# A 16-head decode block on one core: half a run of K per batch held in two PSUM banks between the layers, with exponents and expanded queries moved into other banks

## The chip, the core and the metric

The kernel runs on one of the eight cores of a Trainium2 chip. The metric is device time in microseconds (us), the median of three runs. An execution that the hardware profiler recorded gives the views that are quoted here; instructions in them carry the kernel's line numbers (L673 is line 673 of the kernel before).

## The reference

Eight sequences (batches) decode one token each through two layers of attention and MLP, all in bfloat16. Both layers use the same weights and the same caches of K and V, so each cache is read by layer 0 and again by layer 1. Cut to what matters:

```python
B, D, Hq, Hkv, Sk, Dh = 8, 448, 16, 8, 4096, 256
def _A_ref(x, k_cache, v_cache, wq, wo):            # k_cache, v_cache: (B, Hkv, Sk, Dh)
    q = (x @ wq).reshape(B, 1, Hq, Dh).transpose(0, 2, 1, 3)
    k = jnp.repeat(k_cache, 2, axis=1)
    v = jnp.repeat(v_cache, 2, axis=1)
    p = softmax(einsum("bhqd,bhkd->bhqk", q, k) * Dh ** -0.5)
    return einsum("bhqk,bhkd->bhqd", p, v).reshape(B, 1, Hq * Dh) @ wo

for layer in range(2):
    x = x + _A_ref(layernorm(x), A_k_cache, A_v_cache, A_wq, A_wo)
    x = x + _B_ref(layernorm(x), B_w1, B_w2, B_w3, B_w4)   # an MLP with two layernorms of its own
```

One head of one batch has 4096 x 256 bf16 of K, 2 MB, and as much of V. Eight batches of eight heads are 134 MB of K and 134 MB of V, and layer 1 of a batch needs layer 0 of the whole batch first.

## The kernel before

**Tiles.** SBUF holds NSLOT = 30 slots of 512 KB (4 KB on each of the 128 partitions). A head's K comes as two *runs* of two neighbouring slots (K_RUN = 2, 1 MB, one DMA); a head's V comes as four chunks of one slot. A run's parts are counted in slots, so its `y` is 0 or 2. K lands with keys on partitions and is transposed in place by VectorE in 32 x 32 blocks of 32-bit words, 128x512 words at a time, four instructions for a run (L673). The same instruction applied twice gives the data back. TensorE multiplies the transposed K by the expanded query `qx` into a score bank (L689, `sc`, 32 matmuls a run), then come the softmax (L697 to L723) and the product with V (L753, `v_phase`).

**Kept K.** `KEPT` counts the runs of each batch that stay in their slots, transposed, from layer 0 to layer 1: nine for batch 0, twelve for each of the others, which is all of heads 2 to 7. Heads 0 and 1 (0 to 3 in part for batch 0) load their K again in layer 1. Twelve runs fill 24 of the 30 slots, and six are left to turn over.

**PSUM.** Eight banks: `psS0`, `psS1` for scores, alternating by head in the order of `k_phase` (`n_k % 2`); `psO0`, `psO1` for the product with V; `psM0`, `psM1` for the tail of layer 0 and of layer 1 (projection, MLP, norms, next query); `psX0`, `psX1`. A head's scores take columns 0 to 255 of its score bank. ScalarE writes the exponents from there into `psX0` (L707), VectorE transposes them in place (L712), ScalarE copies the part that is needed into `ring` (L716). All heads use `psX0` for this, one after the other; it is a *strict* resource, whose next writer waits for all earlier users. The expanded query of a batch (`expand`, L502) is made in `psX1`: 16 small matmuls (L512), then four copies into `qx` on VectorE and ScalarE (L521).

**Order of the loads.** `load_order` (L550) lists them, and SP issues them in that order; each waits until the slots that the planner gave it are free. For batch b it lists the K of heads 0 and 1 of layer 0, run by run, between them the K of heads 0 and 1 of layer 1 of batch b-1 (`fr`), then the K of heads 2 to 7 of layer 0. After each run up to two V chunks of layer 0 follow whose scores are due. Then come the rest of layer 0's V, then the V of layer 1 of batch b-1. In this last stretch the tail of layer 0 of batch b runs (`tail`, L789), whose end gives layer 1 its query, and the kept heads are scored for layer 1 (entries "S", 24 us after the last V of layer 0 and then every 2 us, by the planner's clock), which frees their slots. In the text the *K stretch* of a batch is the time in which its K is loaded, and the *V stretch* the time with V loads alone.

**Order on the engines.** `Graph.schedule` (L161) plays the program with estimated durations and fixes each engine's order. An engine that is free takes the ready task with the lowest priority number, and the number is mostly the due time (`at`) plus a constant. A task that takes a slot can begin when a slot is free. SP's queue is looked at first:

```python
        def can(t):
            if not t.allocs:
                return True
            i = t.allocs[0]
            return len(i.pool.free) >= i.reserve + len(t.allocs) and i.pool.find(len(t.allocs)) is not None
```

A task given as a list and marked `whole` is one entry of an engine's order: its instructions run one after the other, each waiting for the end of the one before. Waits between engines, and between tasks, follow from `reads` and `writes` of named resources (`Res`, L72).

## Time and profile before

| | |
|---|---|
| median of 3 runs | 1133.84 us (1133.22 to 1134.58) |
| the profiled execution | 1133.89 us, of which 1132.1 us from the first to the last instruction (the span) |
| loads of K | 163 of 1024 KB, issue to landing 18.8 us in the median |
| loads of V | 512 of 512 KB, 9.1 us |
| busy | PE 698.0 us, VectorE (DVE) 770.5, ScalarE (ACT) 114.5, GpSimd (POOL) 98.3 |
| transposes of K (L673) | 652, 431.1 us busy, 690 ns each |
| scores (L689) | 8192 matmuls |
| exponents (L707), their transposes (L712), copies (L716) | 128 of each, 448, 450 and 213 ns |

How to read the page: it shows busy time in 40 equal slices of the span, as tenths, one row for each engine, one for the DMA engines and one for the GB/s that they moved. The chain of waits is followed back from the last instruction, at each step to what released it; its shares name the engines and lines on that path. A stretch (window) is given in us from the span's start. "To landing" is the time from a load's issue on SP to its last byte: a long one means that many loads stand ahead of it in the queue, not that the load is slow.

### The profile page before, as it was taken

How to read it: one execution, taken by the hardware profiler on the slowest of the kernel's cores; microseconds unless marked ns; L12 is line 12 of the kernel's file. 1: busy time of each engine (PE TensorE's matmuls, PEld its weight loads, DVE VectorE, ACT ScalarE, POOL GpSimd, SP SyncE). 2: the span in 40 equal slices, each digit the busy share in tenths (PEclk: the TensorE clock that was granted, in tenths of full speed). 3: DMA queues.
4: the chain of work that ended last, by engine and by line, in shares of the span. 5: the costliest groups of instructions: out<-in, count | busy, mean ns of one | idle time of the engine just before them, and what ended most of it. 6: DMA issues, size and time to landing. Idle time of an engine off the chain costs nothing.

```text
span 1132.1 us, 41859 instructions
## 1 busy us (share of the span) xinstructions
PE 698.0 (62%) x18716; PEld 466.5 (41%) x18716; DVE 770.5 (68%) x2704; ACT 114.5 (10%) x434; POOL 98.3 (9%) x269
## 2 busy tenths in 40 slices
PE   2534565685557755577555865568555785557775
PEld 2322443353433543345432554335443354334553
DVE  4955799537994379844996459953798438974463
ACT  0100021001110011101111011100111001110110
POOL 0100021001110011100110011100111001100110
PEclk9999965556555555556555565555655555555555
DMA  9999999999999999999999999999999999999993
GB/s 344 415 412 394 411 417 412 405 384 417 415 412 402 404 415 415 403 404 409 415 414 400 402 413 415 413 397 401 416 415 413 395 410 413 416 395 407 409 408 135
DMA packets 101444, 452.63 MB, mean 400 GB/s; under 512 B 11008, under 2 KB 12944, under 8 KB 80016
## 3 DMA queue, kind: packets, MB, share of 16 engines
q1 hardware_dynamic: 101248, 449.96, 99.0%
q8 instruction: 146, 2.39, 0.9%
q14 instruction: 34, 0.28, 0.1%
q10 hardware_dynamic: 16, 0.01, 0.0%
HBM read 449.91 MB, written 0.01 MB: 397 GB/s over the span
## 4 chain that ended last, share of the span: by engine, by line
DVE 35%; DMA 32%; PE 23%; issue 8%; ACT 1%; SPq 0%; POOL 0%; POOLq 0%; ACTq 0%; DVEq 0%
DMA kv<-in_A_v_cache_dram 28%; DVE kv L673 21%; PE psO L753 8%; PE psS L689 7%; PE psM L493 3%; DMA wo_sb<-in_A_wo_dram 2%; DVE psX L712 2%; DVE small L697 2%; PE psM L783 2%; DMA kv<-in_A_k_cache_dram 2%; DVE oX L758 1%; PE psO L765 1%; DVE oT L772 1%; DVE small L885 1%; PE psM L811 1%
## 5 line engine op out<-in xcount | busy, mean ns | idle before, releaser
L673 DVE STREAM_TRANSPOSE kv<-kv 128x512 int32<-128x512 int32 x652 | 431.1, 690 | 16.7 <-DMA kv<-in_A_k_cache_dram 16.4
L689 PE MATMUL psS<-kv,qx 128*8 128x128 bf16 x8192 | 255.0, 296 | 185.1 <-DVE kv L673 88.2
L753 PE MATMUL psO<-kv,ring 128*2 128x256 bf16 x4096 | 288.6, 396 | 102.8 <-DMA kv<-in_A_v_cache_dram 86.7
L689 PEld LDWEIGHTS psS<-kv,qx 128*8 128x8 bf16 x8192 | 196.9, 115 | 243.8 <-DVE kv L673 118.4
L753 PEld LDWEIGHTS psO<-kv,ring 128*2 128x2 bf16 x4096 | 81.0, 94 | 175.2 <-DMA kv<-in_A_v_cache_dram 138.3
L758 DVE STREAM_TRANSPOSE oX<-psO 128x256 f32<-128x256 f32 x128 | 56.2, 439 | 109.6 <-PE psO L753 109.0
L701 POOL PARTITION_ALL_REDUCE small<-small x128 | 46.7, 365 | 712.1 <-DVE small L699 704.8
L783 PE MATMUL psM<-oT,wo_sb 128*128 128x1 bf16 x2048 | 74.0, 166 | 53.7 <-DVE oT L772 41.2
L707 ACT ACTIVATE psX<-psS,small 128x256 f32<-128x256 f32 x128 | 57.4, 448 | 452.2 <-DVE small L703 397.5
L697 DVE TENSOR_REDUCE small<-psS 128x1 f32<-128x256 f32 x128 | 52.4, 409 | 73.1 <-PE psS L689 55.7
L783 PEld LDWEIGHTS psM<-oT,wo_sb 128*128 128x128 bf16 x2048 | 63.9, 104 | 83.3 <-DVE oT L772 65.5
L772 DVE TENSOR_SCALAR oT<-psO,small 64x4 bf16<-64x4 f32 x256 | 55.3, 216 | 47.7 <-PE psO L765 43.0
L721 POOL PARTITION_ALL_REDUCE small<-small x128 | 51.5, 402 | 272.1 <-DVE small L719 237.5
L712 DVE STREAM_TRANSPOSE psX<-psX 128x256 f32<-128x256 f32 x128 | 57.6, 450 | 11.8 <-ACT psX L707 10.3
L765 PE MATMUL psO<-oX,id 128*32 128x4 f32 x1024 | 36.6, 200 | 27.1 <-DVE oX L758 20.7
L765 PEld LDWEIGHTS psO<-oX,id 128*32 128x32 f32 x1024 | 30.2, 145 | 44.7 <-DVE oX L758 35.6
L836 PE MATMUL psM<-small,w_sb 128*128 128x1 bf16 x896 | 30.2, 166 | 22.6 <-DVE small L828 22.3
L836 PEld LDWEIGHTS psM<-small,w_sb 128*128 128x128 bf16 x896 | 27.0, 104 | 37.7 <-DVE small L828 27.6
L716 ACT CAST ring<-psX 128x64 bf16<-128x64 f32 x128 | 27.2, 213 | 149.2 <-DVE psX L712 149.2
L493 PEld LDWEIGHTS psM<-small,wq_sb 128*128 128x128 bf16 x1024 | 30.7, 104 | 17.6 <-issue 12.9
L493 PE MATMUL psM<-small,wq_sb 128*128 128x1 bf16 x1024 | 34.2, 166 | 2.3 <-DVE small L895 1.8
L811 PE MATMUL psM<-small,w_sb 128*128 128x1 bf16 x896 | 28.7, 165 | 8.9 <-DVE small L895 8.9
(91 smaller groups left out, 353.4 us busy)
## 6 DMA issues: line engine op xcount, KB each, us to landing
kv<-in_A_v_cache_dram SPq DMA_DIRECT2D x512, 512.0 KB, 9.1
kv<-in_A_k_cache_dram SPq DMA_DIRECT2D x163, 1024.0 KB, 18.8
wo_sb<-in_A_wo_dram SPq DMA_DIRECT2D x1, 3584.0 KB, 27.1
wq_sb<-in_A_wq_dram SPq DMA_DIRECT2D x3, 1024.0 KB, 7.5
w_sb<-in_B_w_dram SPq DMA_DIRECT2D x1, 1568.0 KB, 18.1
w_sb<-in_B_w_dram SPq DMA_DIRECT2D x3, 448.0 KB, 16.4
wq_sb<-in_A_wq_dram SPq DMA_DIRECT2D x2, 256.0 KB, 11.6
w_sb<-in_B_w_dram SPq DMA_DIRECT2D x2, 112.0 KB, 14.7
```

Source lines behind the costliest of these rows:

```text
L493: last = e.matmul(M[:, base + col * nb:base + (col + 1) * nb], w, xn[:, :, kx], start=(k == 0), stop=(k == NCC - 1))
L673: return e.transpose(ap, ap)
L689: last = e.matmul(S[32 * j:32 * j + 8, w * y:w * y + w], qx[x][:, h, 2 * c + u, :], kt[:, :, c, 8 * j:8 * j + 8, u], start=(c == 0 and u = ...
L697: g.add("dve", lambda e: e.tensor_reduce(pm[par][:, :], S[:, 0:256], axis=AX.X, op=ALU.max), (0.46, 0.33), pr, reads=[rS], writes=[res(f"p ...
L707: g.add("act", lambda e: e.activation(p_ps.rearrange("p (z k y) -> p y z k", z=8, k=8), S[:, 0:256].rearrange("p (y z k) -> p y z k", y=4, ...
L712: g.add("dve", lambda e: e.transpose(p_ps, p_ps), (0.48, 0.38), pr, reads=[rP], writes=[rP])
L753: last = e.matmul(O[32 * j:32 * j + 2, 0:DH], ring[:, pin.slot, i, 2 * a:2 * a + 2], slot_ap(vin)[:, i * DH:(i + 1) * DH], start=(a == 0 a ...
L758: g.add("dve", lambda e: e.transpose(oX[:, :].rearrange("p (c r) -> p c r", r=32), O[:, 0:DH].rearrange("p (a r k) -> p a k r", a=2, k=4)) ...
L765: last = e.matmul(O[32 * a:32 * a + 32, 256:260], id4[:, :], oX[:, :].rearrange("p (a k r) -> p a k r", a=2, k=4)[:, a % 2, :, a // 2], st ...
L772: g.add("dve", lambda e, j=j: e.tensor_scalar(oT[64 * j:64 * j + 64, jb, 4 * h:4 * h + 4], O[64 * j:64 * j + 64, 256:260], rc_ring[64 * j: ...
L783: last = e.matmul(psM[layer][:, c:c + 1], wo_sb[:, c0:c0 + P], oT[:, jb, kt_:kt_ + 1], start=(first and k == 0 and c == 0), stop=False, sk ...
L836: last = e.matmul(M[:, 64 + c:65 + c], w4_sb[:, c0:c0 + P], hT[:, ft:ft + 1], start=(ft == 0), stop=(ft == NFT - 1))
```

## The change

In layer 0 of batches 1 to 7, head 1's second run has its first slot *stashed*: after the transposes in place, two more 128x512 transposes write the slot's content, as it was loaded, into `psX0` and `psX1`, which together hold exactly one slot. It is a whole task on VectorE with priority `at + 10`. In layer 1 the same two transposes bring it back (transposed, as it is needed) into a slot that VectorE's task takes from the pool, with priority `at`; the load for that run fetches only the other slot, 512 KB in place of 1 MB. The two slots of this run are scored by separate tasks of 32 matmuls with 64 columns.

The exponents move to columns 256 to 511 of the head's own score bank, and the expanded query to columns 256 to 383: of the score bank that is next (layer 0), or of the tail's bank `psM0` (layer 1). The score and tail banks are tracked by quarters of 32 partitions (`quads`), and no bank is strict any more. The heads of layer 1 that load again are ordered from the highest down.

```diff
 WO_AT = 11
+STASH = (0, 1, 1, 1, 1, 1, 1, 1)
 AHEAD = (0, 3, 0, 0, 0, 0, 0, 0, 0)
...
-    R["psX0"] = Res(psum=True, strict=True)
     kv_pool = Pool(NSLOT)
...
         return last
-    g.add("dve", c_dve, 3.0, 0, writes=[res("psO0", True), res("psO1", True), res("psS0", True), res("psS1", True),
-                                        res("psM0", True), res("psM1", True), res("xT"), res("wpad"),
+    def quads(bank):
+        return [res(f"{bank}_{a}", True) for a in range(4)]
+    g.add("dve", c_dve, 3.0, 0, writes=[res("psO0", True), res("psO1", True), quads("psS0"), quads("psS1"),
+                                        quads("psM0"), quads("psM1"), res("xT"), res("wpad"),
                                         res("mask"), res("qx0"), res("qx1")])
...
-    def expand(layer, b, prio):
-        X = psX[1]
-        rX = [res(f"psX1_{a}", True) for a in range(4)]
+    def expand(layer, b, X, rX, prio):
         x = layer
...
                 for a in range(4):
-                    last = e.matmul(X[32 * a:32 * a + 32, 384 + 32 * j:416 + 32 * j], eye[:, i0:i0 + 63:2],
+                    last = e.matmul(X[32 * a:32 * a + 32, 256 + 32 * j:288 + 32 * j], eye[:, i0:i0 + 63:2],
                                     q_sb[:, b, :], start=True, stop=True)
             return last
-        g.add("pe", f, (0.37, 0.2), prio, reads=[res(f"q{b}"), res("const")], writes=rX)
+        g.add("pe", f, (0.37, 0.2), prio, reads=[res(f"q{b}"), res("const")], writes=[rX])
         for a in range(4):
...
                 o = qx[x][32 * a:32 * a + 32, :, :, :].rearrange("p h (c s) x -> p s (h c) x", s=4)
-                i = X[32 * a:32 * a + 32, 384:512].rearrange("p (s hc j) -> p s hc j", s=4, j=2)
+                i = X[32 * a:32 * a + 32, 256:384].rearrange("p (s hc j) -> p s hc j", s=4, j=2)
                 o = o[:, :, :, 2 * a:2 * a + 2]
...
-    expand(0, 0, -100)
+    expand(0, 0, psS[0], quads("psS0"), -100)
...
+    def stashed(b, h):
+        if STASH[b] and h == max(i for i in range(HKV) if kept_runs(b, i) < RUNS):
+            return 2 - 2 * kept_runs(b, h)
+        return None
     class Load:
-        def __init__(self, kind, layer, b, h, part):
-            self.kind, self.layer, self.b, self.h, self.part = kind, layer, b, h, part
+        def __init__(self, kind, layer, b, h, part, n=1):
+            self.kind, self.layer, self.b, self.h, self.part, self.n = kind, layer, b, h, part, n
             self.at = None
...
             nonlocal now
-            now += {"K": K_RUN * P * CHUNK * 2 / RATE, "V": P * CHUNK * 2 / RATE, "S": 0.0}[x.kind]
+            now += x.n * P * CHUNK * 2 / RATE if x.kind != "S" else 0.0
             x.at = now
...
         def fresh(layer, b, h):
-            return [Load("K", layer, b, h, y) for y in range(0, 4, K_RUN)
-                    if layer == 0 or y // K_RUN < RUNS - kept_runs(b, h)]
+            return [Load("K", layer, b, h, *((y + 1, 1) if layer and y == stashed(b, h) else (y, K_RUN)))
+                    for y in range(0, 4, K_RUN) if layer == 0 or y // K_RUN < RUNS - kept_runs(b, h)]
...
             l1 = sorted(range(HKV), key=lambda h: -kept_runs(b - 1, h)) if b else []
-            fr = [h for h in l1 if kept_runs(b - 1, h) < RUNS]
+            fr = sorted((h for h in l1 if kept_runs(b - 1, h) < RUNS), reverse=True)
             ks = []
...
     softmax = {}
-    n_k = n_v = 0
...
         S = psS[par]
-        rS = res(f"psS{par}", True)
-        p_ps, rP = psX[0][:, 0:256], res("psX0", True)
+        rS = quads(f"psS{par}")
+        p_ps = S[:, 256:512]
         x = layer
...
         fresh = RUNS - kept_runs(b, h)
-        kts = []
+        pieces = []
         old = kept.pop((b, h), {})
+        def load(y, n, uses):
+            kin = [Inst(kv_pool, u) for u in uses]
+            rk = Res()
+            loads["K", layer, b, h, y] = dma(lambda e: e.dma_start(slot_ap(kin[0], n), k_run(b, h, y, n)),
+                                             n * P * CHUNK * 2, at, [], writes=[rk], takes=kin)
+            done = []
+            for q in range(2 * n):
+                def tr(e, q=q):
+                    ap = slot_ap(kin[0], n).bitcast(i32)[:, q * 512:(q + 1) * 512]
+                    return e.transpose(ap, ap)
+                rKT = Res()
+                g.add("dve", tr, (0.75, 0.615), at + y, reads=[rk], writes=[rKT])
+                done.append(rKT)
+            return y, kin, done
         for y in range(0, 4, K_RUN):
             if y in old:
-                kts.append(old[y])
+                pieces.append(old[y])
+            elif layer == 1 and y == stashed(b, h):
+                back = Inst(kv_pool, 1)
+                rKT = Res()
+                g.add("dve", [
+                    lambda e, q=q: e.transpose(slot_ap(back).bitcast(i32)[:, q * 512:(q + 1) * 512],
+                                               psX[q][:, :].bitcast(i32)) for q in range(2)
+                ], (0.8, 0.65), at, reads=[res("psX0", True), res("psX1", True)], writes=[rKT], takes=[back],
+                    whole=True)
+                pieces += [(y, [back], [rKT]), load(y + 1, 1, [1])]
             else:
                 keep = layer == 0 and y // K_RUN >= fresh
-                kin = [Inst(kv_pool, 2 if keep else 1) for _ in range(K_RUN)]
-                rk = Res()
-                loads["K", layer, b, h, y] = dma(
-                    lambda e, kin=kin, y=y: e.dma_start(slot_ap(kin[0], K_RUN), k_run(b, h, y, K_RUN)),
-                    K_RUN * P * CHUNK * 2, at, [], writes=[rk], takes=kin)
-                done = []
-                for hf in range(2 * K_RUN):
-                    def tr(e, kin=kin, hf=hf):
-                        ap = slot_ap(kin[0], K_RUN).bitcast(i32)[:, hf * 512:(hf + 1) * 512]
-                        return e.transpose(ap, ap)
-                    rKT = Res()
-                    g.add("dve", tr, (0.75, 0.615), at + y, reads=[rk], writes=[rKT])
-                    done.append(rKT)
-                kts.append((kin, done))
+                stash = layer == 0 and y == stashed(b, h)
+                pieces.append(load(y, K_RUN, [2, 1] if stash else [1 + keep] * K_RUN))
                 if keep:
-                    kept.setdefault((b, h), {})[y] = kts[-1]
-        w = K_RUN * 64
-        for y, (kin, done) in enumerate(kts):
+                    kept.setdefault((b, h), {})[y] = pieces[-1]
+                if stash:
+                    _, kin, done = pieces[-1]
+                    g.add("dve", [
+                        lambda e, kin=kin, q=q: e.transpose(
+                            psX[q][:, :].bitcast(i32), slot_ap(kin[0]).bitcast(i32)[:, q * 512:(q + 1) * 512])
+                        for q in range(2)
+                    ], (0.8, 0.65), at + 10, reads=done, writes=[res("psX0", True), res("psX1", True)],
+                        uses=kin[:1], whole=True)
+        for y, kin, done in pieces:
             def sc(e, kin=kin, y=y):
                 last = None
-                kt = slot_ap(kin[0], K_RUN).rearrange("p (i c k u) -> p i c k u", c=4, k=32, u=2)
+                kt = slot_ap(kin[0], len(kin)).rearrange("p (i c k u) -> p i c k u", c=4, k=32, u=2)
                 for c in range(4):
...
                         for j in range(4):
-                            last = e.matmul(S[32 * j:32 * j + 8, w * y:w * y + w], qx[x][:, h, 2 * c + u, :],
-                                            kt[:, :, c, 8 * j:8 * j + 8, u],
+                            last = e.matmul(S[32 * j:32 * j + 8, 64 * y:64 * (y + len(kin))],
+                                            qx[x][:, h, 2 * c + u, :], kt[:, :, c, 8 * j:8 * j + 8, u],
                                             start=(c == 0 and u == 0), stop=(c == 3 and u == 1),
...
                 return last
-            g.add("pe", sc, (1.1, 0.9), at + SC, reads=done + [rq], writes=[rS], uses=kin)
+            g.add("pe", sc, (1.1, 0.9) if len(kin) > 1 else (0.75, 0.55), at + SC, reads=done + [rq], writes=rS, uses=kin)
...
         g.add("dve", lambda e: e.tensor_reduce(pm[par][:, :], S[:, 0:256], axis=AX.X, op=ALU.max), (0.46, 0.33), pr,
-              reads=[rS], writes=[res(f"pm{par}")])
+              reads=rS, writes=[res(f"pm{par}")])
         g.add("dve", lambda e: e.tensor_scalar(pm2[par][:, :], cap[:, :], pm[par][:, 0:1], None, ALU.min), (0.26, 0.12), pr,
...
             ACT.Exp, bias=nb_[par][:, 0:1], scale=INV_SQRT_DH, accum_out=rs[par][:, 0:1]), (0.94, 0.63), pr,
-            reads=[rS, res(f"nb{par}")], writes=[rP, res(f"rs{par}")])
+            reads=rS + [res(f"nb{par}")], writes=rS + [res(f"rs{par}")])
         g.add("dve", lambda e: e.transpose(p_ps, p_ps), (0.48, 0.38), pr,
-              reads=[rP], writes=[rP])
+              reads=rS, writes=rS)
         pin, rin = Inst(pt_pool, 4), Inst(rc_pool, 2)
...
                                       p_ps.rearrange("p (i r) -> p i r", r=32)[:, :, 0:8]), (0.33, 0.3), pr,
-              reads=[rP], writes=[rPT], takes=[pin])
+              reads=rS, writes=[rPT], takes=[pin])
         g.add("dve", lambda e: e.tensor_scalar(rs2[par][:, :], own[:, :], rs[par][:, 0:1], None, ALU.mult), (0.26, 0.12), pr + 1,
...
             return last
-        g.add("pe", wo, (0.75, 0.61), pr + 3, reads=[ro, res("wo"), res("wpad")], writes=[res(f"psM{layer}", True)])
+        g.add("pe", wo, (0.75, 0.61), pr + 3, reads=[ro, res("wo"), res("wpad")], writes=[quads(f"psM{layer}")])
...
         whole = layer == 0 or b == B - 1
-        M, rM = psM[layer], res(f"psM{layer}", True)
+        M, rM = psM[layer], quads(f"psM{layer}")
         rx = res(f"xT{b}") if f"xT{b}" in R else res("xT")
...
             qproj(xa["n3"], 1, b, M, rM, prio, rxc)
-            expand(1, b, prio)
+            expand(1, b, M, rM, prio)
     norm_done = {}
...
                 if x.layer == 0 and begun[0, x.b] == HKV and x.b + 1 < B:
-                    expand(0, x.b + 1, x.at)
+                    expand(0, x.b + 1, psS[n_k % 2], quads(f"psS{n_k % 2}"), x.at)
             if x.kind == "K":
```

More of the change, by code (lines that the diff above doesn't have):

```diff
@@ L151, in add @@
         for r in reads:
-            r.read(t)
+            for q in r if isinstance(r, list) else [r]:
+                q.read(t)
         for w in writes:
-            w.write(t)
+            for q in w if isinstance(w, list) else [w]:
+                q.write(t)
         t.deps.pop(t, None)
@@ L425, in bass_interleave_layers__gqa_block_cached__mixer_s_mlp__decode_kernel @@
             reads=[res("psX0", True)], writes=[res("xT")])
+    n_k = n_v = 0
     def packed_ap(w_sb, n, c, f, m=P):
@@ L801, in tail @@
                 xT[0:m, b, c0:c1], psM[layer][0:m, c0:c1], xT[0:m, b, c0:c1], ALU.add), (0.2, 0.06), prio,
-                reads=[res(f"psM{layer}", True), rx], writes=[nx])
+                reads=[rM, rx], writes=[nx])
         norm_at(tag + "a", M, rM, xb, [None, xa["n2"]], prio, nx, rxb, whole, xn=xa["xn"], xn_res=rxa)
```

## The prediction

> **What bounds the kernel now.** I read the page first: how busy the transfers are over the span, then the chain of waits, then the stretches of one batch by time.
>
> ```profile
> DVE  4955799537994379844996459953798438974463
> ...
> DMA  9999999999999999999999999999999999999993
> GB/s 344 415 412 394 411 417 412 405 384 417 415 412 402 404 415 415 403 404 409 415 414 400 402 413 415 413 397 401 416 415 413 395 410 413 416 395 407 409 408 135
> ...
> HBM read 449.91 MB, written 0.01 MB: 397 GB/s over the span
> ...
> DVE 35%; DMA 32%; PE 23%; issue 8%; ACT 1%; SPq 0%; POOL 0%; POOLq 0%; ACTq 0%; DVEq 0%
> ```
>
> The DMA row is full in 39 of 40 slices, and the rate moves only between about 384 and 417 GB/s. VectorE swings from full to a third of full eight times, once a batch, and the rate hardly follows. The chain names VectorE most, at 35%, so it has to be seen whether VectorE really holds the transfers up. One batch, in three stretches, with the time from issue to landing of the loads issued in the first and the third:
>
> ```profile
> 281.00:319.00 38.00, 22.32 (x648) 16.02 (x645) 37.65 (x117) 4.10 (x16) 3.90 (x11) 0.54 1.02 414
> 319.00:340.00 21.00, 11.27 (x292) 7.20 (x296) 17.96 (x48) 2.34 (x9) 2.27 (x6) 0.50 1.02 412
> 340.00:384.00 44.00, 34.11 (x775) 18.87 (x768) 18.89 (x89) 1.87 (x8) 0.76 (x2) 0.50 1.02 401
> ```
>
> ```profile
> DMA to landing us min/median/max: 15.0/19.6/23.7
> ```
>
> ```profile
> DMA to landing us min/median/max: 5.6/7.0/7.8
> ```
>
> Columns of the first fence: window, length, busy time of PE, weight loads, VectorE, ScalarE, GpSimd, granted clock, DMA share, GB/s. From 281 to 319 VectorE is busy 37.65 of 38 us, and yet the transfers run at 414 GB/s, because loads are issued 15 to 24 us before they land: the queue holds that much work. In the V stretch (340 to 384) VectorE is 43% busy, the lead is 7.0 us, and the rate is 401. There 24 of the 30 slots hold kept K and six are left: 6 x 0.524 MB at 401 GB/s is a cycle of 7.85 us, of which 7.0 us is flight and 0.85 us use. So the time is bytes over rate all along, and the rate is a little lower where only six slots turn over. VectorE's 35% of the chain is the path that hands slots back while the queue is still deep.
>
> **What goes.** Seven of the eight batches (STASH is 0 for the first) load half a run of K less in layer 1: 7 x 524,288 bytes = 3.67 MB. These loads stand in the K stretch, where the rate is 414: 3.67 MB / 414 GB/s = **8.9 us**. (At 397, the mean over the span, 9.2; at 417, 8.8.) The loads' number stays at 163; seven become 512 KB. With them go seven times two 128x512 transposes of the fresh half, which the restore replaces by as many.
>
> The halves are smaller loads than before. But the V loads have this very size, 512 KB, and between 319 and 340, when seven of the eight issues are V and the queue is still deep, the rate is 412 beside 414. So I count nothing (bounds: 0, and 7 x 0.524 MB x (1/401 - 1/414) = 0.3 us). The Trainium skill, "DMA: Bandwidth & Descriptors", section "Rules for kernel authors", asks for at least 1 MiB in one DMA. As an estimate, if a half came at the 341 GB/s that the page's bandwidth table gives for 1 MB, seven would cost 1.9 us more, and the sum below would be 1128. The trace's 412 decides against that.
>
> **What is added on VectorE.** Each stash is two 128x512 transposes out of a slot into PSUM, 14 in all. The row of the 128x512 transpose inside SBUF has 690 ns. From PSUM there are only 128x256 rows: 450 ns in place, 439 into SBUF; two of these hold 512 columns, so a restore's transpose lies between 690 and 900 ns. I take 700, since 256 columns more cost the SBUF form little over 0.27 us per 256 by its own length (0.45 + 0.27 = 0.72). Both are whole tasks: the second transpose waits for the first's end, where back to back two take 1.22 us in the chain. So a stash costs 1.4 us, a restore 0.2 us more than the pair it replaces: 1.6 us a batch, **11 us in all, hidden** by the lead of 15 to 24 us. What it does cost: the K stretch's VectorE work grows by 1.6 us while its transfers shrink by 1.27, so the deep queue ends up to 2.9 us earlier and that much more of the batch runs at 401 rather than 414: 2.9 x 3.1% = 0.09 us, times 7 = **0.6 us**. Bounds: 0 (the restore may fall where VectorE is 43% busy) and 11 us if all of it were uncovered.
>
> The stashed half's slot is held longer, since the stash has the load's due time plus 10 us: one slot of 30 for about 10 us, while the lead is 20 us. Nothing; were the lead short there, 10 us at the six-slot rate would be 0.3 us a batch, 2 us in all.
>
> **What is moved.** Exponents go from the one strict bank psX0 to the upper half of the head's own score bank. Gone is the wait of one head's exponent for the previous head's ring copy; new is that the next head but one, which uses the same bank, waits for the ring copy instead of the exponent. From exponent's end to copy's end is at least a transpose and a copy, 0.45 + 0.21 = 0.66 us; in the scoring of the kept heads around 255 to 281 single heads show 0.5, 1.4 and once 4.0 us (exponent over at 267.9, copy at 272.0). Behind PE's scoring stand, in PE's order, the PV and wo matmuls. In the K stretch a head comes every 5 to 10 us and two banks give twice that: covered. In the kept heads' scoring, one head in about 4 us, it can delay the release of slots: up to 6 us a batch, in which the queue stays at the six-slot rate: 6 x 3.1% x 7 = 1.3 us; I take a third, **0.4 us**. Below nothing too: the strict bank's wait goes, but no transfer waited for it visibly; 0 to -0.5. ScalarE now reads and writes one bank; VectorE's transpose that does so has 450 ns and the one from PSUM into SBUF 439, so this is some 10 ns of an engine that is 10% busy.
>
> The expanded queries move into the next score bank (layer 0) or into the tail's own bank (layer 1): the same 16 matmuls and four copies of 0.26 to 0.28 us, once a batch, with PE waiting about 1 us at most in front of the kept heads' scoring, when no run of fresh K stands behind it. PE gains 7 x 32 matmuls, since the half that is stashed and the half that is loaded are scored apart, with 64 columns each; 32 with 128 columns take 1.02 us in the chain, so at most 7 us at 59% busy PE in the K stretch. Layer 1's fresh heads change places (1 before 0; in batch 0, 3 2 1 0 for 3 0 1 2): the same loads. All nothing. The start (to 46 us) and the end (the DMA share of 1110 to 1120 is 0.32, so the last landing is near 1113) are untouched.
>
> **Sum.** 1133.9 - 8.9 + 0.6 + 0.4 = **1126.0 us**. It is made against the profiled execution, 1133.89 us with a span of 1132.1, which agrees with the median of the runs, 1133.84.
>
> **Rivals.** *A lost slot (slower).* The restore waits for the stash alone, and the planner hands out a slot as soon as VectorE has nothing more urgent and one is free. If that is before the V stretch, the half sits in one of the six slots for it, and the lead becomes that of five: with the use of 0.85 us and the shortest landing seen, 5.6 us, five slots cycle in 6.45 us, which is 406 GB/s and no loss; with the landing staying at 7.0 us it is 5 x 0.524 / 7.85 = 334, some 9 us in each 44. Between them I take 385, a step a little larger than that from 414 to 401, over the V stretch and 11 us on its sides: 55 us x 4% = 2.2 us a batch, 15 us in all: **1141 us**. It decides from 7.9 / 7 = 1.1 us a batch, a rate under 391 over the 44 us. For it: nothing in the code holds the restore back until its due time. Against: single slots go to V loads first, which stand at the head of the queue, VectorE is full until the last pair of kept K is issued, and where the kept heads are scored slots come free in fours. 14%.
>
> *VectorE becomes the bound (about no change).* If the lead is used up before the K stretch ends, the 11 us are paid: 1126.0 - 0.6 + 11 = 1136, and with four fifths of them **1134**. For: VectorE has 35% of the chain and is 99% busy for 38 us. Against: the shortest lead there is 15.0 us, and 2.9 us comes off it. 6%.
>
> *The score banks (slower or a smaller gain).* If the kept heads' scoring sets when slots return, six heads with 0.66 us over two banks are 2 us a batch, 14 in all: **1139**; when half is covered, 1133. For: PE already waits there (3.13 and 2.74 us at 260 and 267). Against: the lead rises from 7 to 20 us in just that time. This is also what the Trainium skill would expect ("Perfetto Trace Analysis", section "Matmuls": independent groups should rotate through PSUM banks so that emptying one overlaps the next's matmuls). By that rule fewer free banks slow the matmuls; no row here shows that PE's pace sets the rate at that place. 4%.
>
> *The half isn't saved* (stash and restore do not spare the load): excluded by the list of loads, apart from a reordering that costs as much. Dips such as 361 GB/s at 240 to 250 us and 365 at 1010 to 1020 cost some 1.3 us each; a new plan may add or remove two or three.
>
> **Chances.** Forecast 76%, with its own range of 1123 to 1131: the terms reach from -9.2 - 0.5, with one dip gone (-1.3), to -8.9 + 0.3 for the halves, + 2 for the two queue terms and + 3.9 for three dips. The rivals take 24%: A 14, VectorE 6, banks 4. The range for 8 in 10 is 1123 to 1132, which takes in the forecast's own and a part of the second and third rival. A measurement of this kernel tells 0.2% (2.3 us) from no change: faster 0.78 (the forecast and the cheap end of the banks), same 0.07, slower 0.15.
>
> **What would show it.** Right: 446.2 MB read; 638 in-place transposes and 28 with PSUM; batch period shorter by about 1.1 us; the DMA row still full; the lead in the K stretch 12 us or more; the V stretch at 400 GB/s with a landing of 7 us. Wrong: a landing of 6 us or less and a rate under 391 in the V stretch (the slot was taken early); a lead near 6 us or a DMA share under 1 with VectorE full (VectorE binds); loads waiting for the scores between the V stretch and the K stretch (the banks). Restores that run right behind their stash on VectorE, far ahead of their scores, would show the first rival's mechanism even where it costs little.

## The result, and the profile after

The changed kernel takes **1128.33 us** (median of 4 runs, 1128.03 to 1128.88), the kernel before on the same chip 1133.62: a ratio of 0.9953 [0.9935, 0.9970]. The forecast was 1126.0, in a range of 1123 to 1132. The profiled execution took 1128.03 us, 5.9 us less than the one of before (1133.89), where 7.9 us less was forecast. The page of the changed kernel:

```profile
DVE  4945799537994489844996469963798438984463
...
DMA  9999999999999999999999999999999999999992
GB/s 345 415 412 391 405 413 412 409 390 415 415 413 399 399 414 415 405 405 407 414 414 399 402 407 414 414 401 405 414 416 406 396 402 415 413 393 407 411 408 115
...
HBM read 446.24 MB, written 0.01 MB: 396 GB/s over the span
...
DVE 38%; DMA 27%; PE 25%; issue 8%; ACT 1%; SPq 0%; POOL 0%; POOLq 0%; DVEq 0%; ACTq 0%
```

The traffic is 3.67 MB less, as it should be; the DMA row is as full as before. The chain gives the transfers 27% in place of 32 and the engines the rest, and the last slice moves 115 GB/s in place of 135: the transfers are over sooner, by more than the kernel is. The same three stretches of one batch, with the landing times of the first and the third (columns as in the prediction):

```profile
281.00:319.00 38.00, 22.21 (x624) 16.29 (x616) 37.58 (x117) 4.10 (x16) 4.17 (x12) 0.54 1.02 414
319.00:339.00 20.00, 11.61 (x300) 6.91 (x304) 16.99 (x46) 2.33 (x9) 1.90 (x5) 0.50 1.02 413
339.00:383.00 44.00, 33.75 (x765) 18.60 (x757) 18.69 (x89) 1.85 (x7) 0.75 (x2) 0.50 1.02 398
```

```profile
DMA to landing us min/median/max: 13.6/19.6/22.9
```

```profile
DMA to landing us min/median/max: 5.6/6.9/7.5
```

The rates are those of before within 3 GB/s (401 became 398 in the V stretch), and the landing times are close to before's: 13.6 us at least in the K stretch (15.0 before), 6.9 in the median in the V stretch (7.0). The instructions that stash and restore are the only ones that touch both `psX` and a slot. Groups of the tile psX; the columns are count, then the least, median and longest ns, then the first and the last start:

```profile
L709 DVE STREAM_TRANSPOSE psX<-kv x14: 675/724/728, 143.1 to 965.8; 128x512 int32<-128x512 int32 x14
L695 DVE STREAM_TRANSPOSE kv<-psX x14: 672/716/718, 252.3 to 1054.1; 128x512 int32<-128x512 int32 x14
```

The first stash runs at 143.1 us and its restore at 252.3, 109 us later, when the kept heads' scoring gives slots back. It was not taken early.

**Where the time went.** Two moments can be read in any trace of this kernel: when the layer-1 query of a batch is ready (the end of its copy into `q_sb`), which tells how far the stream of loads has come, and when the last load lands. After minus before, in us:

| batch | 0 | 1 | 2 | 3 | 4 | 5 | 6 | 7 | last landing |
|---|---|---|---|---|---|---|---|---|---|
| before at | 131.1 | 248.0 | 382.1 | 516.1 | 650.0 | 784.8 | 919.9 | 1053.6 | 1116.3 |
| after | +0.4 | 0.0 | -0.7 | -1.3 | -2.4 | -4.1 | -5.6 | -6.4 | -8.1 |

The stream is 8.1 us shorter, a little over 1 us for each half that is not loaded. The seventh half would be loaded after the last query (that batch's layer-1 loads of K are issued from 1057 us on, before the change), so by that query six are saved, and it comes 6.4 us sooner. The kernel ends 13.1 us after the last product with `wo`, in both. What differs lies between the last landing and that product: 2.7 us before, **4.9 us** after. TensorE at the end, before and then after; columns are start, length, engine, line, operation, tiles and shape, count, and in brackets the idle time ahead of the row and what ended it:

```profile
1115.12 0.59 PE L753 MATMUL psO<-kv,ring 128*2 128x256 bf16 x8 [0.48 <-DMA kv<-in_A_v_cache_dram]
1116.36 0.59 PE L753 MATMUL psO<-kv,ring 128*2 128x256 bf16 x8 [0.65 <-DMA kv<-in_A_v_cache_dram]
...
1118.40 0.59 PE L783 MATMUL psM<-oT,wo_sb 128*128 128x1 bf16 x16 [0.60 <-DVE oT L772]
```

```profile
1099.50 0.83 PE L816 MATMUL psM<-oT,wo_sb 128*128 128x1 bf16 x26 [2.13 <-issue]
...
1105.71 0.59 PE L816 MATMUL psM<-oT,wo_sb 128*128 128x1 bf16 x16 [0.16 <-DVE oT L805]
...
1109.13 0.58 PE L816 MATMUL psM<-oT,wo_sb 128*128 128x1 bf16 x16 [0.16 <-DVE oT L805]
...
1109.64 1.45 PE L786 MATMUL psO<-kv,ring 128*2 128x256 bf16 x24
...
1112.54 0.58 PE L816 MATMUL psM<-oT,wo_sb 128*128 128x1 bf16 x16 [0.60 <-DVE oT L805]
```

Before, each group of eight matmuls waits for a V chunk that is just landing, and the last `wo` product comes 2.0 us behind the last of them. After, nothing at the end waits for a load: the last head's chunks have all landed (1108.3) when TensorE takes up 24 of its 32 matmuls in one go at 1109.6, and a head follows a head by 3.4 us (1105.71 to 1109.13 to 1112.54), where its four loads take 5.0 us. From the end of the last expansion of a query into `qx` (1055.7 us before, 1049.6 after) to the end of the last `wo` product TensorE and its partners need 63.3 us before and 63.5 us after; from the last query of the table it is 65.4 and 66.0. Before, that was just as long as the loads took. After, the query comes 6.4 us sooner and the loads 8.1 us sooner, and the end follows the query.

Part of the 63 us is time in which TensorE waits for nothing that the profile's semaphores show ("issue"). Its waits in the last stretch, before (1056 to 1119.5) and after (1050 to 1113.5): us in total, times, longest:

```profile
PE psS L689 <- issue: 6.4, 3, 2.8
...
PE psM L783 <- issue: 1.9, 1, 1.9
...
PE psO L753 <- DMA kv<-in_A_v_cache_dram: 1.1, 2, 0.6
...
PE psO L765 <- issue: 0.8, 1, 0.8
```

```profile
PE psS L722 <- issue: 9.3, 5, 2.6
PE psO L786 <- issue: 2.6, 2, 1.7
...
PE psM L816 <- issue: 2.1, 1, 2.1
...
PE psO L786 <- DMA kv<-in_A_v_cache_dram: 0.7, 1, 0.7
```

The "issue" rows add up to 9.1 us before and 14.0 after. They are TensorE waiting for its own instructions. Counted through the whole trace after (matmuls, weight loads and the 146 instructions of TensorE's queue that only wait or drain), all 44 such gaps of over 0.4 us begin at the same place modulo 256, within one. The page lists a queue of 148 instruction packets, 2.42 MB, so 16.4 KB each: one packet for about every 257 of TensorE's 38,026 instructions. The trace also holds the times of these packets, and each of the 44 gaps ends 1.2 to 1.6 us after one of them has landed, as do all 34 gaps of before; of the 307 other waits of that length in the trace after, 23 do. So TensorE waits there for its next block of code: up to 2.9 us at 44 places after (65.0 us in all), up to 3.6 us at 34 before (61.6 us).

The packet that ends such a wait starts 3.7 us in the median after TensorE has entered the block ahead of it and takes 1.1 us. With the time from its landing to the end of the wait, that makes 6.2 us for a block that ends in a wait (the median; 32 of the 44 take 6.0 to 6.5 us), where blocks without a wait take 7.5 us. So these waits come where TensorE would go through a block in less, and a deep queue of loads alone does not bring them: in the K stretch from 281 to 319, with a median lead of 19.6 us (lead is the time from a load's issue to its landing), the longest such wait is 0.5 us, in the V stretch 0.7. Behind the last query TensorE goes through its code as fast as it comes: eight blocks in a row, from 1048.0 to 1099.5 us, end in a wait. Ahead of the end the lead of the loads can cover such waits; at the end it can't.

### The profile page after: what moved, and what is told of

The parts are those of the page before. It is cut to its first block, busy times and chain, and to the rows that moved or that the text cites. A ratio compares the mean times of both kernels' runs of the same rounds, so it can differ in the third digit from the quotient of the medians.

```text
span 1126.2 us, 42325 instructions
## 1 busy us (share of the span) xinstructions
PE 701.9 (62%) x18940; PEld 472.0 (42%) x18940; DVE 779.5 (69%) x2718; ACT 114.1 (10%) x434; POOL 97.6 (9%) x269
## 3 DMA queue, kind: packets, MB, share of 16 engines
q8 instruction: 148, 2.42, 0.9%
## 4 chain that ended last, share of the span: by engine, by line
DVE 38%; DMA 27%; PE 25%; issue 8%; ACT 1%; SPq 0%; POOL 0%; POOLq 0%; DVEq 0%; ACTq 0%
DMA kv<-in_A_v_cache_dram 23%; DVE kv L682 22%; PE psO L786 9%; PE psS L722 7%; PE psM L502 3%; DVE small L730 2%; DVE psS L745 2%; DMA wo_sb<-in_A_wo_dram 2%; PE psM L816 2%; DMA kv<-in_A_k_cache_dram 2%; DVE oT L805 2%; DVE oX L791 1%; PE psM L844 1%; PE psO L798 1%; PE psM L869 1%
## 5 line engine op out<-in xcount | busy, mean ns | idle before, releaser
L682 DVE STREAM_TRANSPOSE kv<-kv 128x512 int32<-128x512 int32 x638 | 422.4, 690 | 15.0 <-DMA kv<-in_A_k_cache_dram 14.6
L722 PE MATMUL psS<-kv,qx 128*8 128x128 bf16 (+1 forms) x8416 | 255.3, 294 | 167.7 <-DVE kv L682 68.0
L786 PE MATMUL psO<-kv,ring 128*2 128x256 bf16 x4096 | 285.3, 395 | 111.7 <-DMA kv<-in_A_v_cache_dram 77.5
L722 PEld LDWEIGHTS psS<-kv,qx 128*8 128x8 bf16 x8416 | 200.4, 115 | 215.2 <-DVE kv L682 87.7
L740 ACT ACTIVATE psS<-psS,small 128x256 f32<-128x256 f32 x128 | 57.4, 448 | 432.4 <-DVE small L736 389.1
L745 DVE STREAM_TRANSPOSE psS<-psS 128x256 f32<-128x256 f32 x128 | 56.6, 443 | 8.3 <-ACT psS L740 7.1
L869 PEld LDWEIGHTS psM<-small,w_sb 128*128 128x128 bf16 x896 | 27.4, 104 | 35.6 <-DVE small L861 23.9
L749 ACT CAST ring<-psS 128x64 bf16<-128x64 f32 x128 | 27.1, 212 | 134.2 <-DVE psS L745 126.2
L844 PE MATMUL psM<-small,w_sb 128*128 128x1 bf16 x896 | 29.0, 166 | 13.6 <-DVE small L928 13.3
L844 PEld LDWEIGHTS psM<-small,w_sb 128*128 128x128 bf16 x896 | 26.4, 104 | 24.7 <-DVE small L928 18.1
```

Of the source, the lines that this page charges most:

```text
L682: return e.transpose(ap, ap)
L722: last = e.matmul(S[32 * j:32 * j + 8, 64 * y:64 * (y + len(kin))], qx[x][:, h, 2 * c + u, :], kt[:, :, c, 8 * j:8 * j + 8, u], start=(c = ...
L745: g.add("dve", lambda e: e.transpose(p_ps, p_ps), (0.48, 0.38), pr, reads=rS, writes=rS)
L786: last = e.matmul(O[32 * j:32 * j + 2, 0:DH], ring[:, pin.slot, i, 2 * a:2 * a + 2], slot_ap(vin)[:, i * DH:(i + 1) * DH], start=(a == 0 a ...
L844: last = e.matmul(M[:, 32 + ft:33 + ft], w, xa["n2"][:, 0, cx:cx + 1], start=(c == 0), stop=(c == NCC - 1))
L869: last = e.matmul(M[:, 64 + c:65 + c], w4_sb[:, c0:c0 + P], hT[:, ft:ft + 1], start=(ft == 0), stop=(ft == NFT - 1))
```

## The experiments

The ratio and its interval always compare with the kernel before on the same chip. "Query to wo" is the time from the end of the last expansion of a query into `qx` to the end of the last `wo` product (63.5 us in the profile of the changed kernel), "landing to wo" from the last landing. One profile of each run is read. The first two theories: **E**, the end belongs to TensorE, which is late because of the order of V that it is given there; and **W**, the work of stash and restore on VectorE costs the two missing microseconds.

**1 and 2. Order of the last V, on the kernel after and on the kernel before.**

```diff
-                l1 = fr + [h for h in l1 if h not in fr]
+                l1 = [h for h in range(HKV - 1, -1, -1) if h not in fr] + fr
```

> The changed kernel with one line more: in the last stretch the V of layer 1 of the last batch is loaded in the order in which its heads are scored (7 to 2, then 1 and 0) and not 1, 0 first. Theory E (the end): the changed kernel's loads end 8.0 us earlier than before, but TensorE has eight heads of product with V left when the last scores are made, at 3.0 to 3.4 us a head, and ends 2.1 us later behind the last landing than the kernel before did. With the order of the scores this backlog is worked off while loads still run: 1128.3 - 2.1 = 1126.2 us, the last wo product 2.7 us behind the last landing. Theory W (the missing 2.6 us are paid along the way, by VectorE's added work or by the shared score banks): no change, 1128.3 +- 0.5.

> The kernel before with the same line. Theory E: before the change the last product with V waited for its load (0.65 us at 1116.4), so the order of V has nothing to give: 1133.6, between -0.7 and +0.3 us. A gain of 2 us here as well would mean that the order is worth the same with and without the change, and that it does not explain what is missing. Theory W: no change too.

After: 1128.04 us, 0.9947 [0.9935, 0.9960]; the profile is of the slowest of its five runs, 1130.35. Before: 1134.59, 1.0003 [0.9994, 1.0012]. So the order gains nothing on either, and E in the form that blamed it has fallen. With the loaded heads' V last, the last scores come 9 us later (1091.5 in place of 1082.6), and query to wo is still 62.2 us. Which head stands last does not hold the end; that the amount of work behind the query and its gaps do is the reading that is left, and these two runs do not test it.

**3. Without the last batch's stash.** `STASH = (0, 1, 1, 1, 1, 1, 1, 0)`.

> The changed kernel without the stash of the last batch (STASH 0 for it): 1.27 us of loads come back at the end. Theory E: TensorE's backlog, not the loads, sets the end, and the backlog begins with the last scores, which wait for the chain of softmaxes rather than for their K: 1128.3 to 1128.8 us. Theory W: each batch's stash is worth the same, (1133.6 - 1128.3) / 7 = 0.76 us or a little over it: 1129.1 to 1129.6 us.

1127.39 us, 0.9940 [0.9927, 0.9952]. Half a megabyte more is loaded, and it costs nothing; W expected 0.8 us or more, E up to 0.5. TensorE at the end:

```profile
1109.23 0.59 PE L786 MATMUL psO<-kv,ring 128*2 128x256 bf16 x8 [0.37 <-DMA kv<-in_A_v_cache_dram]
...
1111.28 0.59 PE L816 MATMUL psM<-oT,wo_sb 128*128 128x1 bf16 x16 [0.60 <-DVE oT L805]
```

The loads end 0.9 us later, TensorE waits for the last of them again, and landing to wo is back at 2.7 us. So the seventh half is worth nothing: it saves loads that the end doesn't wait for. The run leaves out that batch's restore too, and its code lies differently: from the query of the table to the last `wo` product it takes 64.9 us, 1.1 less than the changed kernel (66.0). So the second chain is no fixed length.

**4. The moves alone.** `STASH` all 0: exponents and queries share the banks, and nothing is stashed.

> The changed kernel with STASH 0 throughout: exponents and expanded queries in the score and tail banks, heads of layer 1 from the highest down, no stash, no restore, all loads whole. The record's terms: 0.4 us slower than before by the longer hold of the score banks, 1134.0 us. Theory E: the same, 1133.3 to 1134.5. Theory W with the banks as the cost: 2 us or more slower, 1135.6 us. Theory W with VectorE as the cost: 1133.6.

1134.87 us, 1.0007 [0.9998, 1.0016]: +0.8 us, where the prediction had put 0.4; the interval takes in no cost at all. Queries come between 0.4 us earlier and 1.0 us later than before, with no growth from batch to batch, and landing to wo is 2.7 us. The banks are not where the end's 2.2 us went.

**5 and 6. The changed kernel again, and a later restore.** The restore comes in the last batch at 1053.4 us, 1.4 us in the middle of a softmax chain. Theory **R**: this is what delays the end. A third read, of the sum that an earlier head's softmax leaves (`db`), makes it wait until that head is through:

```diff
-reads=[res("psX0", True), res("psX1", True)], writes=[rKT], takes=[back],
+reads=[res("psX0", True), res("psX1", True), res(f"db{par}")], writes=[rKT], takes=[back],
```

> The changed kernel once more, beside the next three on one chip: 0.9953 of before, and at the end the last wo product 4 to 5 us behind the last landing, as in its first profile (4.9), not 2.7 as before the change and without the last stash.

> The changed kernel, whose restore also waits for the second reduction of the head two places earlier in the scoring order, so that it does not run between two steps of the first kept head's softmax. Theory R (the restore's 1.4 us on VectorE delay the last batch's scores, and these set the end): the end is 1.1 to 1.4 us earlier than in the changed kernel, its last wo product under 3.8 us behind the last landing. Theory F (at the end TensorE waits for its own code, at each 256th of its instructions, 14.0 us in the last 75 us against 9.1 us before the change): no change beyond 0.6 us either way, unless the waits for code fall elsewhere.

The changed kernel: 1129.44 us (1127.11 to 1131.94), 0.9958 [0.9944, 0.9972]; its profiled execution, the fastest of the five at 1127.11, has queries at +0.1, -0.1, -0.9, -1.6, -2.3, -3.5, -5.7, -6.5, the last landing at -7.4 and landing to wo of 3.2 us. So the same program ends once 2.2 us and once 0.6 us later behind its loads than the kernel before. With the later restore, which runs at 1076.3 us in the last batch: 1128.12, 0.9946 [0.9933, 0.9960], landing to wo 4.1 us where R wanted under 3.8. The median is 1.3 us better, which is what R expected, but the intervals overlap: R is neither shown nor excluded.

**7. No stash, no restore, and the load still halved.** The scores of the run's first slot are computed from its second slot's K, so the output isn't the reference's; all else is there.

> The changed kernel without the stash and the restore: the run's first slot is not brought back, and its scores are computed from the second slot's K in its place. Bytes, TensorE's work and the banks are those of the changed kernel; VectorE does four transposes a batch less. It prices all that VectorE's added work costs. The record's terms: 0.6 us faster than the changed kernel (from 0 to 1). Theory R: 1.1 to 1.4 us more, so 1.7 to 2.0 us. Theory F: 0.6 us, and the last wo product still 4 to 5 us behind the last landing.

1127.47 us, 0.9938 [0.9925, 0.9950]. The median is 2.0 us under the changed kernel's on the same chip, where the prediction's terms had 0.6 and R 1.7 to 2.0; the intervals just overlap. The profiles show less: the last query comes 7.4 us sooner than before in place of 6.4, and this 1.0 us is there already at batch 0's query, before the first stash. By the query from which one counts, the 28 instructions, 19.9 us of VectorE, cost the stream between nothing and 0.6 us. Landing to wo is 3.9 us. So W does not explain the late end: take all the added work away, and the end still comes 1.2 us later behind the loads than before. That the work costs up to 2 us in all is not excluded.

**8, 10 and 11. Shifting the code.** Theory **F**: TensorE's waits for its code fall on other work in every program; what moves them can move the time. 64 small matmuls (128 instructions with their weight loads) into `psX1`, which nobody reads, shift all later places by half a block; 128 of them by a whole one, which gives the same places as no shift. In `shift_128` they stand at the start, in the other two behind a head of batch 0:

```diff
+        for part in range(4 if (layer, b, h) == (0, 0, 3) else 0):
+            def idle(e):
+                for i in range(16):
+                    last = e.matmul(psX[1][0:32, 8 * i:8 * i + 8], eye[:, 0:32], eye[:, 0:8], start=True, stop=True)
+                return last
+            g.add("pe", idle, (0.7, 0.6), at, reads=[ro], writes=[res("psX1", True)])
```

> The changed kernel with 64 more small matmuls and their weight loads in the first 60 us, in a bank that nothing uses then: TensorE's later instructions move by 128 places, half of the 256 between two waits for code. The loads and all other work stay. Theory F: the waits fall on other work, and the end moves by 0.5 to 2 us, while the last landing stays within 0.5 us. Theory R: no change beyond 0.3 us.

> The changed kernel with the 64 small matmuls and weight loads of shift_128 placed where nothing waits for TensorE, behind the fourth head's product in batch 0. TensorE's later instructions move by 128 places, as there. Theory F (the end and single places in the stream hang on where TensorE's waits for code fall): not the changed kernel's time, but 1 to 4 us above or below it, with the last wo product at another distance from the last landing. Theory S (what shift_128 lost, it lost by the delay at the start, 0.8 us, and what follows from it): the changed kernel's time within 0.7 us.

> The same with 128 small matmuls and weight loads: a shift by 256 places, a whole period, so that the later waits for code fall on the same work as in the changed kernel. Theory F: the changed kernel's time within 0.7 us, though this has twice the added work of shift_128_later. Theory S: twice what shift_128_later differs by.

128 at the start: 1132.87 us, 0.9989 [0.9980, 0.9998]. 128 later: 1132.44, 0.9986 [0.9977, 0.9994]. 256 later: 1130.15 (1128.33 to 1133.53), 0.9960 [0.9946, 0.9974], as the changed kernel alone (0.9958). Half a block costs 3.4 and 2.3 us (beside 1129.44 and beside the whole block, each on its own chip), a whole one, with twice the work, nothing that can be told: F holds. Its expectation for `shift_128` was a miss all the same: the last landing was to stay within 0.5 us, and it comes 3.2 us later than in the changed kernel's first profile. Where half a block costs, in the trace of `shift_128_later`:

```profile
156.75 0.60 PE L722 MATMUL psS<-kv,qx 128*8 128x128 bf16 x16 [2.82 <-issue]
...
166.78 0.69 PE L722 MATMUL psS<-kv,qx 128*8 128x128 bf16 x17 [2.85 <-issue]
...
176.87 0.70 PE L722 MATMUL psS<-kv,qx 128*8 128x128 bf16 x18 [2.94 <-issue]
```

In the changed kernel's trace TensorE has no such wait between 150 and 180 us, nor has it in that of `shift_256_later`; `shift_128` has three there, 9.2 us in all. Three windows, first of `shift_128_later`, then of the changed kernel:

```profile
170.00:180.00 10.00, 4.33 (x148) 3.82 (x152) 6.97 (x26) 1.29 (x7) 1.90 (x5) 0.50 1.02 415
...
200.00:210.00 10.00, 5.87 (x172) 3.89 (x165) 8.85 (x24) 1.00 (x5) 1.15 (x3) 0.50 0.93 325
210.00:220.00 10.00, 6.23 (x148) 2.88 (x136) 3.89 (x16) 1.39 (x5) 0.75 (x2) 0.50 0.91 324
```

```profile
170.00:180.00 10.00, 6.28 (x200) 4.87 (x188) 9.90 (x30) 1.55 (x6) 1.50 (x4) 0.54 1.02 415
...
200.00:210.00 10.00, 6.04 (x152) 3.19 (x152) 6.37 (x19) 1.56 (x6) 0.75 (x2) 0.50 1.02 408
210.00:220.00 10.00, 6.13 (x116) 2.28 (x116) 2.62 (x13) 0.04 (x1) 0.40 (x1) 0.50 1.03 408
```

Three waits of 2.9 us in one K stretch hold TensorE, and VectorE has work for only 6.97 of 10 us in place of 9.90. At 170 to 180 the queue still covers that (415 GB/s); 30 us later 20 us run at 325 GB/s in place of 408, which is some 4 us of transfers. That the late scores gave slots back late is the reading of these windows. Batch 1's layer-1 query comes 1.8 us later than in the changed kernel, the last one 3.2 us, and landing to wo is 6.6 us.

**9. The first rival made to happen.** The restore gets priority -1000, so that it takes its slot at once.

> The changed kernel, whose restore has the most urgent priority, so that it follows its stash within a few us and the half sits in a slot through the whole V stretch, which turns over five slots. It prices the record's first rival. The record: 385 GB/s in the V stretch in place of 401 and about 15 us in all, so 1143 to 1144 us beside 1128 to 1129 for the changed kernel. Bounds: no loss if the flight shrinks to 5.6 us, 1128; 334 GB/s and some 60 us if it stays at 7.0 us, 1190.

1147.09 us (1136.67 to 1151.83), 1.0096 [1.0059, 1.0132]. The restores run from 145.0 us on, 1.7 us behind their stashes, and five slots are left in the V stretch (window 345 to 389, and the landing there):

```profile
345.00:389.00 44.00, 33.99 (x780) 19.50 (x772) 16.50 (x79) 0.73 (x3) 0.26 (x1) 0.50 0.98 373
```

```profile
DMA to landing us min/median/max: 4.6/6.0/9.2
```

373 GB/s beside 398, landing after 6.0 us beside 6.9. The five runs lie 15 us apart; the profiled one took 1141.61.

**12. Seven halves that all count.** Batch 0's half is stashed in place of the last one's, with the late restore: `STASH = (1, 1, 1, 1, 1, 1, 1, 0)`.

> The changed kernel with the stash in batches 0 to 6 and none in the last, and the later restore of restore_late. The last batch's saving comes after its layer-1 query is ready, and from there to the last wo product the kernels take 62 to 63.5 us whatever was saved; batch 0's saving comes before it. Theory E in its present form: 1.0 to 1.3 us faster than the changed kernel, 0.994 - 0.001 = 0.993 of before (1126.2 where before is 1134.2). If every batch's stash counts alike: the time of restore_late.

1128.47 us (1127.71 to 1128.89), 0.9951 [0.9938, 0.9963], and not the 0.993 that was expected. Landing to wo is 2.7 us, as hoped, but what batch 0's half saves is lost again by the next query:

```profile
130.00:140.00 10.00, 6.70 (x226) 4.85 (x226) 8.62 (x25) 1.60 (x6) 1.15 (x3) 1.00 0.74 266
```

In the changed kernel this window runs at 381 GB/s. From 120 to 150 us 11.0 MB are moved there and 12.0 in the changed kernel, which is 2.4 us at 415 GB/s, more than the 1.3 us that the half saves. SP's waits for slots that scoring gives back (L722, 125 to 145 us) are 15.9 us in place of 12.9; why the scores are later there was not followed further. A further 1.7 us is lost against the changed kernel between the queries of batches 2 and 7 (-0.2 becomes +1.5), and that was not followed either. No version was clearly better than the changed kernel: the best ratios, 0.9940 and 0.9938 (the second with a wrong output), have intervals that overlap with its own.

## Why the prediction was right, and where it was off

The sign, the range and the mechanism of the stream were right; the forecast was 2.3 us low, and one step, the end, was wrong.

- *Bytes over rate, 8.9 us, and the two queue terms, together 7.9 us:* the last landing came 8.1 us sooner in the first profile and 7.4 in the second of the same program, at rates within 3 GB/s of before. Halves of 512 KB in a deep queue cost nothing that shows. The prediction's estimate from the Trainium skill's rule of at least 1 MiB ("DMA: Bandwidth & Descriptors", "Rules for kernel authors") would have taken 1.9 us of this; the trace does not show that loss.
- *VectorE, 11 us hidden, 0.6 us in the queue:* a stash's transpose takes 724 ns, a restore's 716, where 700 was put; 14 of each are 19.9 us. Without them the stream gains 0.6 us at most in the profiles, and the median is 2.0 us lower. Most of the work is hidden; the size of the 0.6 us is not shown.
- *The banks, 0.4 us:* 0.8 us with the moves alone, in an interval that takes in 0. The Trainium skill's rule that independent groups rotate through PSUM banks ("Perfetto Trace Analysis", "Matmuls"), on which the prediction's third rival drew, has room for no more than that here. So the two small terms agree with the runs in their sum, at the last landing; that each was right is not shown, and part of the agreement may be luck.
- *The lost slot, 1141 us:* it did not happen, for the reason given (slots come free in fours where the kept heads are scored), as far as the time of the restores shows. Forced, it cost 17.7 us over the changed kernel's 1129.44 on the other chip by the medians and some 15.6 by the ratios, where 15 over the forecast was the price; 373 GB/s where 385 was taken.
- *The step that failed:* "The start (to 46 us) and the end (the DMA share of 1110 to 1120 is 0.32, so the last landing is near 1113) are untouched." The last landing of before is at 1116.3 us, not near 1113. And the end was taken to begin there, because before the change the last V chunk and TensorE arrive together. There were two chains of equal length: the loads' end, and the last query plus TensorE's work behind it. The change takes 8.1 us off the first, but only 6.4 off the second, since the seventh half lies behind that query. The second now ends last, and landing to wo grows from 2.7 to 4.9 us: 8.1 - 2.2 = 5.9 us gained, and 5.9 measured. In the second profile it grows by 0.6 only, so the size of this step is between 0.6 and 2.2 us. Experiment 3, in which the seventh half is loaded again at no cost and landing to wo falls back to 2.7, fits this; it also takes away a restore and moves the code, so it does not prove it alone. In the five profiles of this document in which the loads end last (the kernel before, experiments 2, 3, 4 and 12) landing to wo is 2.67 us each time; in the nine others it lies between 3.2 and 6.6. The prediction's seven times 1.27 us was a count of bytes, not of when each is needed.
- *Dips that a new plan may add or remove:* allowed for in the range, and their cause is now known in part. Waits for code lie differently in each program, and half a block of shift costs 2.3 to 3.4 us, about half of the whole gain. Why runs of one and the same program spread from 1127.1 to 1131.9 us is not settled, nor whether a restore in the softmax chain costs the end anything.

## What to carry to other kernels

A load that is saved is worth its time only if what ends last waits for it: before counting bytes, follow the second chain at the end too, from its last start to the end, and ask by how much it is shorter than the first. When a stream and an engine end together, as here, a change to the one alone pays only until the other is late. And compare versions of a kernel with long engine programs with care: 128 instructions more moved the time by 0.2 to 0.3% here, for reasons that have nothing to do with their work, which a second shift by a whole block of code can tell. In this kernel, TensorE's instructions behind the last query are themselves a cost, at some 6.2 us for 256; no run here has fewer of them.

## What the runs showed that was not expected

TensorE's code comes in blocks of 256 instructions, and a block takes 6.2 us where TensorE waits for it: 2.82, 2.85 and 2.94 us of waiting in one K stretch of `shift_128_later`, 61.6 us in an execution of the kernel before and 65.0 after, some of it covered by the lead of the loads. The Trainium skill ("Runtime: NRT & Kernel Launch", "Instruction fetch mechanics") has the same block, 256 instructions in 16 KiB, and calls the cost of crossing it mostly hidden. That agrees with the trace after in number, since 44 of some 148 crossings show a wait of over 0.4 us; in time it does not where TensorE would go through a block in less than 6.2 us.

VectorE's 32-bit transpose costs nearly the same wherever it reads or writes here: 690 ns in SBUF, 724 into PSUM, 716 out of it, for 128x512. So two PSUM banks are a usable store for 512 KB between two stages, at 1.4 us in and 1.4 us out; of the 19.9 us that this takes here, at most some 2 show in the time.
